# First MLP weights walked forwards and backwards, a planner that counts changes of matmul kind, and six pairs' sums on TensorE

## The chip, the cores and the metric

One core of one Trainium2 chip runs the whole program. The metric is the device time of one execution in microseconds (us), and the median over the runs is what is compared.

## The reference

Three stages follow each other. First comes soft-capped attention over 4 batches, 12 heads, 448 positions and head size 64:

```python
scores = scale * np.matmul(q, k.transpose(0, 1, 3, 2))
scores = cap * np.tanh(scores / cap)
attn = np.exp(scores - scores.max(-1, keepdims=True))
attn = attn / (attn.sum(-1, keepdims=True) + 1e-09)
attn_out = np.matmul(attn, v)
```

Then the 1792 tokens of width 768 go through a first MLP, `h = x @ w_in` (768 to 2048), `g = h * clip(h + 3, 0, 6) / 6`, `x2 = g @ w_out`. Last, each token is given to one of eight experts, greedily by its logits `x2 @ w_gate` with 224 tokens for each expert, and goes through that expert's two matrices with a relu between them.

## The kernel before, in words

The work is done in a first, planned part (attention, `x @ w_in`, the activation, the logits) and two later parts (`g @ w_out` with the routing beside it, and the experts). The change touches the planned part alone.

**Slots.** A pair is two heads of one batch; there are 24 pairs `g`, six for each batch. A slot is half a pair: two of the four chunks of 112 keys. `slot(h)` issues, for slot h: the scores (`score`, 12 matmuls of 64 rows each into the PSUM tile `sc`), the tanh and the exp on ScalarE into `P`; and for slot h-1: `av` (8 matmul instructions of 64 columns each into `po`) and `uadd`, the VectorE addition of the two chunks of `P`, which makes `u0` in the first half of a pair and `sb` in the second. For pairs from `G3 = 12` on, the second half adds `u0` as well (two additions, "whole").

**Sums and division.** Once for every two pairs, `fin_sum` multiplies `u0` and `sb` with a column block of ones (`ones`, four groups of 32 columns side by side) into the PSUM tile `ms`: 16 matmul instructions where both halves are summed on TensorE, 8 where VectorE has added them already. VectorE transposes the sums, inverts and transposes back; the result goes to DRAM (`RD`) and returns spread over the partitions (`rb`). `fin_x` multiplies the attention output `xu` by it and splits it into a high and a low part, `XH` and `XL`, which are `X[b]` of the batch. The list `FIN` says how many slots behind the two are issued (2 and 3).

**First MLP.** `m1a_pieces(b)` works through 16 tiles `f` of `w_in` in three parts of six matmuls each into `ph` (two PSUM banks). Part p needs pairs 2p and 2p+1 of `X[b]`. In batch 0 each weight tile is decoded from 64-bit numbers on VectorE (`decode`), split into a high and a low part (`wsplit`), and twelve of the sixteen (`STR`) are written to DRAM `WD` and read back by `wload` for each later batch into a ring of three buffers `ws`. The four others (`RES`) stay in `wr`. `lg_mm` sums logits from four tiles of `g` (`ms`); `wog_pieces` makes `w_out @ w_gate` on the way.

**Order.** Every operation is given to `Plan.add` with an engine, a cost and what it reads and writes; `merge` interleaves the streams by share, which fixes each operation's position. `Plan.run` then emits the program: each engine takes, among the operations that are ready by the costs, the one of the lowest position. `LAG = 6` is the number of slots by which a batch's MLP follows its attention. The engines' queues, SyncE's DMA queue too, run in the order emitted.

Of the kernel before, what the change touches and what calls it, by code (L numbers as in the profile page):

```python
# [33 lines left out]
class Plan:  # L34
# [6 lines left out]
    HOP = 0.15  # L41
    LAND = 2.0
# [15 lines left out]
    def add(self, eng, cost, fn, r=(), w=(), kb=0, after=()):  # L58
# [7 lines left out]
        for key in w:  # L66
# [5 lines left out]
            if own not in self.first:  # L72
                self.first[own] = me
                if name in self.rings:
                    deps.update(self.users.get((name, i - self.rings[name]), ()))
                    if i > 0:
                        deps.add(self.first[name, i - 1])
# [6 lines left out]
        self.ops.append((eng, cost, fn, deps, kb))  # L84
# [5 lines left out]
    def run(self):  # L90
# [12 lines left out]
        total = wire = 0.0  # L103
        for _ in range(n):
# [8 lines left out]
            _, cost, fn, _, kb = self.ops[i]  # L113
            ready[eng].remove(i)
            free[eng] = t + cost
            end = t + cost
# [14 lines left out]
def fused_kernel(ctx: ExitStack, tc: tile.TileContext, q, k, v, cap, w_in, w_out, w_gate, w1, w2,  # L131
# [22 lines left out]
    ones = cst.tile([CP + 1, 32], F32, name="ones")  # L154
    nc.gpsimd.memset(ones, 1.0)
    SB = []
    for i in range(2):
        SB.append(cst.tile([CP + 1, 2, S], F32, name=f"sb{i}"))
    guard = cst.tile([CP + 1, 1], F32, name="guard")[96:CP + 1]
# [30 lines left out]
                 "xu": 3, "ms": 1, "R": 2, "r14": 1, "rb": 2, "X": 2, "wraw": 2, "wy": 2, "ws": 3, "wot": 1, "ph": 2, "r": 1,  # L190
# [35 lines left out]
    def score(h):  # L226
# [15 lines left out]
        add("PE", 1.5, mm, r=[("KH", g), ("KL", g), ("QH", g), ("QL", g)], w=[("sc", 4 * g + c) for c in cc])  # L242
# [9 lines left out]
    G3 = 12  # L252

    def uadd(h):
# [6 lines left out]
        def go():  # L261
            u = SB[g % 2] if s_ else put(ap_, key, [CP, 2, S])
            T[key] = u
            if s_ and g >= G3:
                nc.vector.tensor_add(u[:CP], T["u0", g], T["P", 4 * g + 2])
                nc.vector.tensor_add(u[:CP], u[:CP], T["P", 4 * g + 3])
            else:
                nc.vector.tensor_add(u[:CP], T["P", 4 * g + 2 * s_], T["P", 4 * g + 2 * s_ + 1])
# [4 lines left out]
    def av(h):  # L273
# [12 lines left out]
        add("PE", 1.8, mm, r=[("tv", g)] + [("P", 4 * g + c) for c in cc], w=[("po", g)])  # L286
# [10 lines left out]
    def fin_sum(g):  # L297

        m, i = plan.next("ms"), g // 2
        halves = (1,) if g >= G3 else (0, 1)  # L300

        def mm():
            p = bank(("ms", m))
            for s_ in halves:
                for n in range(4):
                    u = T[("u0", "sb")[s_], g - 1 + n // 2]
                    r = CP + s_
                    nc.tensor.matmul(p[32 * n:32 * n + 32, :S], ones[:r], u[:r, n % 2], start=(s_ == halves[0]), stop=(s_ == 1))
        add("PE", 0.85 * len(halves), mm, r=[(("u0", "sb")[n], x) for n in halves for x in (g - 1, g)] + [("guard", 0)], w=[("ms", m)])
# [9 lines left out]
        add("DVE", 1.35, rec, r=[t], w=[R])  # L319
# [27 lines left out]
    def slot(h):  # L347
# [3 lines left out]
        av(h - 1)  # L351
        for t, fn in FIN:
# [3 lines left out]
        uadd(h - 1)  # L356
# [6 lines left out]
    FIN = ((2, fin_sum), (3, lambda g: fin_x(g - 1)), (3, fin_x))  # L363
# [21 lines left out]
    def wog_pieces():  # L385
# [8 lines left out]
        def tr(f, part):  # L394
# [11 lines left out]
            def out_():  # L406
                if i == 0 and part == 0:
                    put(dcp, ("wot", q_), [128, KD, 512])
                nc.scalar.activation(T["wot", q_][:, d0:dn, i * 128:(i + 1) * 128],
                                     T["ms", m][:, :(dn - d0) * 128].rearrange("p (d f) -> p d f", f=128), AF.Copy)  # L410
            add("ACT", 0.5, out_, r=[("ms", m)], w=[("wot", q_, f, part)])

        def mm(q_):
            m, m2 = plan.next("ms"), plan.next("ms")

            def go():
                p = bank(("ms", m))
                for d in range(KD):
                    for i in range(4):
                        nc.tensor.matmul(p[32 * i:32 * i + 32, :128], wgt[:, d, :],  # L420
                                         T["wot", q_][:, d, i * 128:(i + 1) * 128], start=(d == 0), stop=(d == KD - 1))
            add("PE", 1.0, go, r=[("wot", q_), ("wgt", 0)], w=[("ms", m)])
            c = ("wot", q_, "c")
            add("DVE", 0.3, lambda: nc.vector.tensor_copy(T["wot", q_][:, 0, :128], T["ms", m][:, :128]), r=[("ms", m)], w=[c])
            add("PE", 0.2, lambda: nc.tensor.transpose(bank(("ms", m2))[:, :128], T["wot", q_][:, 0, :128], ident),
# [6 lines left out]
        for f in range(NF):  # L432
            for part in range(len(PARTS)):
                r.append((300, lambda f=f, part=part: tr(f, part)))
            if f % 4 == 3:
                r.append((1500, lambda q_=f // 4: mm(q_)))
        return r

    W = {}

    def wput(f, key):
        if f in WD:
            T[key] = [m1p.tile([128, KD, 128], F32R, name="ws" + n, bufs=3) for n in "hl"]
        else:
            T[key] = [m1p.tile([128, KD, 128], F32R, name=f"wr{n}{f}", bufs=1) for n in "hl"]

    def wload(b, f):
        if f in WD:
            W[f] = key = ("ws", plan.next("ws"))

            def go():
                wput(f, key)
                for i in range(2):
                    nc.sync.dma_start(T[key][i].bitcast(F32), WD[f][i])
            add("SP", 0.7, go, r=[("WD", f)], w=[key], kb=768)

    def wsplit(f):

        y = decode(w_in[f], [128, KD, 128], lambda t: t)
        W[f] = key = ("ws", plan.next("ws")) if f in WD else ("wr", f)  # L460

        def high():
            wput(f, key)
# [8 lines left out]
    def lg_mm(b, tiles, first, pool):  # L472
# [6 lines left out]
        add("PE", 0.9, mm, r=[g for _, g in tiles] + [("wog", tiles[0][0] // 4)], w=[("ms", m)])  # L479
# [49 lines left out]
    def m1a_pieces(b, logits):  # L529
        gs = {}  # L530

        def mm(f, part):
            key = ("ph", NF * b + f)
            if part == 0 and f + 2 < NF:
                wload(b, f + 2) if b else wsplit(f + 2)
# [13 lines left out]
            add("PE", 1.24, go, r=xs + [w], w=[key])  # L549
            if part < 2:  # L550
                return
            n = NF * b + f
# [670 lines left out]
```

## Time and profile before

| | us |
|---|---|
| median of three runs | 1034.09 (1032.96 to 1037.63) |
| profiled execution, its own time | 1036.34 |
| its span, first to last instruction | 1034.6 |
| planned part, to the first matmul of `g @ w_out` | 473.9 |

The profile's time axis starts with the first instruction. "Busy" is the time in which an engine has an instruction under way; a TensorE matmul stays on record for longer than it holds up the next, so starts tell more than durations. The granted clock is a share of 2.4 GHz. "PE" is TensorE's matmul, "PEld" its weight load, "DVE" VectorE, "ACT" ScalarE, "SPq" SyncE's DMA queue. A release "<-" names what ended an idle time.

### The profile page before, as it was taken

The numbers are of one execution on the slowest core, as the hardware profiler recorded it, in microseconds if no ns is written. First come the engines' busy times: TensorE is split into PE (matmuls) and PEld (weight loads), VectorE is DVE, ScalarE is ACT, GpSimd is POOL, SyncE is SP. The second block draws the span as 40 slices with busy tenths as digits, with TensorE's granted clock in tenths as the row PEclk, the third lists the DMA queues.
The fourth block names the chain that finished last, engine by engine and source line by source line (L and its number), as shares of the span: only waits on it lengthen the run. The fifth ranks groups of instructions, "written<-read, shape, count | busy, mean of one in ns | idle before, by whom it ended". The sixth has DMA issues, their size and how long they took to land.

```text
span 1034.6 us, 17381 instructions
## 1 busy us (share of the span) xinstructions
PE 996.5 (96%) x6337; PEld 819.0 (79%) x6337; DVE 740.7 (72%) x1318; ACT 510.9 (49%) x868; POOL 133.0 (13%) x146
## 2 busy tenths in 40 slices
PE   6988999999999999999999999999989999999997
PEld 3434667676756678878789989998979999999996
DVE  6999888687776545447898779877337777777673
ACT  7988877776767633432110101010136665566652
POOL 0000000000000000000000000000024555545542
PEclk9999999999999999999999999999999999999999
DMA  7577999999987679996445646547948777667760
GB/s 221 154 238 237 302 342 312 382 333 318 357 286 228 199 232 339 343 315 194 151 139 141 170 108 180 135 138 226 317 170 271 232 232 242 227 223 235 244 225 29
DMA packets 120182, 242.26 MB, mean 234 GB/s; under 512 B 23392, under 2 KB 85904, under 8 KB 120096
## 3 DMA queue, kind: packets, MB, share of 16 engines
q1 hardware_dynamic: 115504, 225.08, 65.7%
q0 software_dynamic: 3328, 11.01, 3.9%
q10 hardware_dynamic: 1264, 5.05, 1.5%
q8 instruction: 50, 0.82, 0.3%
q14 instruction: 36, 0.29, 0.1%
HBM read 181.19 MB, written 59.91 MB: 233 GB/s over the span
## 4 chain that ended last, share of the span: by engine, by line
PE 70%; DVE 17%; DMA 7%; issue 3%; ACT 1%; SPq 1%; POOLq 0%; ACTq 0%; POOL 0%; DVEq 0%
PE py L1128 13%; PE x L1011 12%; PE ph L1083 7%; PE ph L545 7%; PE ph L547 6%; PE ph L546 6%; PE po L284 4%; DVE g L832 4%; PE ph L1085 4%; PE sc L241 3%; DVE g L830 3%; DMA wraw<-in_moe_w_in 1%; PE ro L840 1%; DMA gh<-gh 1%; PE ms L478 1%
## 5 line engine op out<-in xcount | busy, mean ns | idle before, releaser
L1011 PE MATMUL x<-woh,gh 128*128 128x384 f32 x448 | 125.4, 342 | 2.0 <-DMA gh<-gh 2.0
L1011 PE MATMUL x<-wol,gh 128*128 128x384 f32 x448 | 123.2, 336 | 0.0
L1011 PE MATMUL x<-woh,gl 128*128 128x384 f32 x448 | 122.2, 336 | 0.0
L545 PE MATMUL ph<-XH,wsh 128*128 128x448 f32 x288 | 110.6, 384 | 1.5 <-DMA wsh<-wd 1.2
L547 PE MATMUL ph<-XH,wsl 128*128 128x448 f32 x288 | 105.6, 367 | 0.5 <-DMA wsl<-wd 0.5
L546 PE MATMUL ph<-XL,wsh 128*128 128x448 f32 x288 | 105.3, 366 | 0.0
L245 ACT ACTIVATE P<-sc,rcap 112x896 f32<-112x896 f32 x96 | 92.2, 1005 | 12.4 <-PE sc L241 9.3
L249 ACT ACTIVATE P<-P,capt 112x896 f32<-112x896 f32 x96 | 95.6, 1045 | 0.0
L284 PE MATMUL po<-P,tv 112*64 112x448 f32 x384 | 84.3, 559 | 5.6 <-ACT P L245 3.2
L1011 PEld LDWEIGHTS x<-woh,gh 128*128 128x128 f32 x448 | 80.2, 188 | 5.8 <-DMA gh<-gh 2.9
L1011 PEld LDWEIGHTS x<-woh,gl 128*128 128x128 f32 x448 | 81.5, 188 | 1.0 <-issue 0.6
L1011 PEld LDWEIGHTS x<-wol,gh 128*128 128x128 f32 x448 | 81.5, 188 | 0.6 <-issue 0.6
L554 ACT ACTIVATE r<-ph,three 128x448 f32<-128x448 f32 x64 | 40.6, 634 | 73.2 <-PE ph L547 73.2
L545 PEld LDWEIGHTS ph<-XH,wsh 128*128 128x128 f32 x288 | 54.1, 188 | 27.3 <-issue 18.4
L556 DVE SCALAR_TENSOR_TENSOR g<-r,ph 128x448 f32<-128x448 f32 x64 | 39.5, 618 | 41.3 <-ACT r L554 41.2
L832 DVE TENSOR_SCALAR g<-mrb,m 112x1344 bf16<-112x1344 f32 (+11 forms) x105 | 68.5, 664 | 0.0
L1083 PE MATMUL ph<-xe,woh 128*128 128x448 f32 x186 | 60.8, 383 | 1.4 <-DVE xe L1069 1.0
L1105 DVE SCALAR_TENSOR_TENSOR hl<-ht,hh 128x224 fp32r<-128x224 f32 x64 | 39.9, 624 | 29.3 <-ACT hh L1104 27.9
L284 PEld LDWEIGHTS po<-P,tv 112*64 112x64 f32 x384 | 23.5, 137 | 46.1 <-issue 27.5
L748 POOL IOTA icol<- 112x112 f32 x1 | 0.2, 230 | 461.3 <-PE ph L546 461.3
L547 PEld LDWEIGHTS ph<-XH,wsl 128*128 128x128 f32 x288 | 54.1, 188 | 5.9 <-DMA wsl<-wd 1.2
L546 PEld LDWEIGHTS ph<-XL,wsh 128*128 128x128 f32 x288 | 54.2, 188 | 3.7
(211 smaller groups left out, 2243.9 us busy)
## 6 DMA issues: line engine op xcount, KB each, us to landing
wol<-in_moe_w SPq DMA_DIRECT2D x32, 768.0 KB
woh<-in_moe_w SPq DMA_DIRECT2D x31, 768.0 KB
gh<-gh SPq DMA_DIRECT2D x64, 224.0 KB
gl<-gl SPq DMA_DIRECT2D x64, 224.0 KB
wsh<-wd SPq DMA_DIRECT2D x36, 384.0 KB
wsl<-wd SPq DMA_DIRECT2D x36, 384.0 KB
wraw<-in_moe_w_in SPq DMA_DIRECT2D x16, 768.0 KB
wraw<-in_moe_w_out SPq DMA_DIRECT2D x16, 768.0 KB
```

Of the source, the lines that this page charges most:

```text
L245: add("ACT", 0.96, lambda i=i: nc.scalar.activation(put(ap_, ("P", i), [CP, 2, S]), T["sc", i][:CP, :, :S], AF.Tanh, scale=rcap[:CP]), r=[ ...
L249: add("ACT", 0.99, lambda i=i: nc.scalar.activation(T["P", i], T["P", i], AF.Exp, scale=capt[:CP]), r=[("P", i), ("capt", 0)], w=[("P", i)])
L284: nc.tensor.matmul(T["po", g][64 * j:64 * j + 64, :S], T["tv", g][:, j, c, :], T["P", 4 * g + c][:, j], start=(c == 0), stop=(c == NC - 1))
L545: nc.tensor.matmul(p, wh[:, d], XH[:, d], start=(d == 0), stop=False)
L546: nc.tensor.matmul(p, wh[:, d], XL[:, d], start=False, stop=False)
L547: nc.tensor.matmul(p, wl[:, d], XH[:, d], start=False, stop=(d == KD - 1))
L554: add("ACT", 0.64, lambda: nc.scalar.activation(put(m1p, r_, [128, S]), T[key][:, :S], AF.Relu, bias=three), r=[key], w=[r_])
L832: nc.vector.tensor_scalar(g[:, s_:], mr[:, s_:], mj, None, op0=OP.is_le)
L1011: nc.tensor.matmul(X2[g, i, hf][:, :HW], a, w[:, hf * HW:(hf + 1) * HW], start=bool(f == 0 and first), stop=bool(f == NF - 1 and last))
L1083: nc.tensor.matmul(p[:, :2 * TE], wh[:, d, fs], X2[:, d].rearrange("p a t -> p (a t)"), start=(d == 0), stop=False)
L1085: nc.tensor.matmul(p[:, :TE], wl[:, d, fs], X2[:, d, 0], start=False, stop=(d == KD - 1))
L1128: nc.tensor.matmul(PY[e][2 * t + hf][:CP, :384], a[:, f, tsl], w[:, f % 2, hf * 384:(hf + 1) * 384], start=bool(f == 0 and first), stop=bo ...
```

## The change

1. **Weights by turns.** `order(b)` walks the tiles forwards in even batches and backwards in odd ones. The last three streamed tiles of a batch stay in their buffers, which are now three named ones (`ws0` to `ws2`) handed out from a list `FREE`; a load is issued when a buffer's tile was used for the last time (`wused`). Each later batch loads 9 streamed tiles and not 12. `wog_pieces` goes backwards too, and the logits of batch 1 follow their tiles by two matmul parts fewer.
2. **Planner.** Operations on TensorE carry a kind: 0 for the MLP and the transposes, 1 for scores, 2 for `av`, 3 for sums and logits. A change of kind costs `TURN`; an operation of the kind now running (or any of kinds 1 to 3 while one of these runs) goes first if its position is less than `KEEP` behind the lowest one ready. The costs of TensorE's operations are lowered to leave the change out.
3. **Sums of six pairs on TensorE.** For pairs 0 to 5 (`G0 = 6`) `uadd` adds nothing on VectorE: for each slot four matmuls (eight instructions) of `ones` with the two chunks of `P` go straight into two of the four column groups of `ms`, which gathers two pairs over four slots. `G3` goes from 12 to 6, so pairs 6 to 11 have their third addition on VectorE and half the sum matmuls.
4. **Guard.** The small addend of the denominator is no longer an extra row of `sb`, but is added to the transposed sums.
5. **Positions.** `FIN` is 1 slot for all three steps, `LAG` is 3, and `uadd` is issued before them. The pool `late` is closed at `turn_att`.

```diff
+    TURN = 0.19
+    KEEP = 40
...
-                    i = min(i for i in c if at[i] <= t)
+                    now = [i for i in c if at[i] <= t]
+                    i = min(now)
+                    if eng == "PE" and self.ops[i][5] != was:
+                        same = [x for x in now if self.ops[x][5] == was or (was and self.ops[x][5])]
+                        if same and min(same) < i + self.KEEP:
+                            i = min(same)
...
+            if eng == "PE":
+                cost += self.TURN * (kind != was)
+                was = kind
...
-        add("PE", 1.5, mm, r=[("KH", g), ("KL", g), ("QH", g), ("QL", g)], w=[("sc", 4 * g + c) for c in cc])
+        add("PE", 1.2, mm, kind=1, r=[("KH", g), ("KL", g), ("QH", g), ("QL", g)], w=[("sc", 4 * g + c) for c in cc])
...
-    G3 = 12
+    G3 = 6
+    G0 = 6
+    MS = {}
...
+        if g < G0:
+            n0 = 2 * (g % 2)
+            if h % 4 == 0:
+                MS[g // 2] = ("ms", plan.next("ms"))
+            m = MS[g // 2]
+
+            def mm():
+                p = bank(m) if h % 4 == 0 else T[m]
+                for c in (2 * s_, 2 * s_ + 1):
+                    for j in range(2):
+                        nc.tensor.matmul(p[32 * (n0 + j):32 * (n0 + j) + 32, :S], ones, T["P", 4 * g + c][:, j],
+                                         start=(c == 0), stop=(c == NC - 1))
+            add("PE", 1.5, mm, kind=3, r=[("P", 4 * g + 2 * s_), ("P", 4 * g + 2 * s_ + 1)], w=[m])
+            return
...
-            nc.vector.reciprocal(r, y[:, :, 0])
+            nc.vector.tensor_scalar(r, y[:, :, 0], guard, None, op0=OP.add)
+            nc.vector.reciprocal(r, r)
...
-    FIN = ((2, fin_sum), (3, lambda g: fin_x(g - 1)), (3, fin_x))
+    FIN = ((1, fin_sum), (1, lambda g: fin_x(g - 1)), (1, fin_x))
...
+    def wused(b, f):
+
+        if f not in WD:
+            return
+        o = [x for x in order(b) if x in WD]
+        n = o.index(f)
+        if b < B - 1 and n >= len(o) - 3:
+            return
+        FREE.append(int(W[f][0][2:]))
+        if b and n + 3 < len(o):
+            wload(o[n + 3])
...
-    add("DVE", 1.6, guards, r=[("gexp", 0)], w=[("guard", 0)])
...
-    LAG = 6
+    LAG = 3
```

## Rows read from the trace of the kernel before

**Rows 1.** The page's first part: busy time, share of span, instructions of each engine.
```profile
PE 996.5 (96%) x6337; PEld 819.0 (79%) x6337; DVE 740.7 (72%) x1318; ACT 510.9 (49%) x868; POOL 133.0 (13%) x146
```

**Rows 2.** Windows by stretch: length, each engine's busy us (instructions), granted clock, DMA share.
```profile
4.50:23.50 19.00, 14.80 (x72) 6.74 (x72) 14.83 (x26) 15.16 (x18) 0.00 (x0) 0.94 0.82 257
23.50:59.00 35.50, 33.57 (x214) 15.74 (x212) 32.87 (x52) 33.07 (x39) 0.00 (x0) 0.98 0.55 169
59.00:104.00 45.00, 38.91 (x235) 20.43 (x234) 42.50 (x63) 39.41 (x52) 0.00 (x0) 1.00 0.76 235
104.00:364.00 260.00, 256.32 (x1631) 177.42 (x1630) 192.92 (x287) 191.45 (x281) 0.00 (x0) 1.00 0.89 307
364.00:474.00 110.00, 106.90 (x549) 86.08 (x547) 50.58 (x81) 40.49 (x66) 1.63 (x12) 1.00 0.86 299
```

**Rows 3.** Timeline of TensorE, 305 to 310 us: start, us, line, tiles, count.
```profile
305.69 0.36 PE L546 MATMUL ph<-XL,wsh 128*128 128x448 f32 x1
305.89 0.37 PE L547 MATMUL ph<-XH,wsl 128*128 128x448 f32 x1
306.19 0.46 PE L241 MATMUL sc<-QH,KH 64*112 64x448 f32 x2
306.48 0.37 PE L241 MATMUL sc<-QH,KL 64*112 64x448 f32 x2
...
307.59 1.72 PE L284 MATMUL po<-P,tv 112*64 112x448 f32 x8
309.24 0.96 PE L308 MATMUL ms<-sb,ones 113*32 113x448 f32 x8
```

**Rows 4.** Timeline, 27 to 29 us: one `fin_sum` of two halves and the next score.
```profile
27.11 0.96 PE L308 MATMUL ms<-u,ones 112*32 112x448 f32 x8
...
27.89 0.94 PE L308 MATMUL ms<-sb,ones 113*32 113x448 f32 x8
...
28.76 0.46 PE L241 MATMUL sc<-QH,KH 64*112 64x448 f32 x2
```

**Rows 5.** Timeline of TensorE, 9 to 12 us: the first change of kind.
```profile
10.88 1.41 PE L284 MATMUL po<-P,tv 112*64 112x448 f32 x6
```

**Rows 6.** Timeline of TensorE, 470 to 475 us: the last change of kind.
```profile
473.52 0.65 PE L497 MATMUL ms<-ident,lacc 128*112 128x128 f32 x4 [0.86 <-DVE lacc L487]
```

**Rows 7.** Timeline of all engines and SyncE's queue, 56 to 88 us.
```profile
56.19 1.98 ACT L249 ACTIVATE P<-P,capt 112x896 f32<-112x896 f32 x2
...
63.30 1.08 DVE L268 TENSOR_TENSOR sb<-P 112x896 f32<-112x896 f32 x1
...
66.32 0.96 PE L308 MATMUL ms<-u,ones 112*32 112x448 f32 x8
...
69.06 0.67 DVE L311 STREAM_TRANSPOSE R<-ms 128x448 f32<-128x448 f32 x1
...
77.91 1.11 SPq L329 DMA_DIRECT2D rb<-rd  x2
```

**Rows 8.** Timeline of VectorE: the last piece of `X[0]`.
```profile
86.82 0.62 DVE L345 TENSOR_TENSOR XL<-xu,XH 128x448 fp32r<-128x448 f32 x1
```

**Rows 9.** Groups by line on VectorE, 5 to 104 us: busy, mean ns, idle before.
```profile
L268 DVE TENSOR_TENSOR u<-P 112x896 f32<-112x896 f32 x10 | 10.7, 1070 | 0.0
...
L378 DVE SCALAR_TENSOR_TENSOR wy<-wraw,wy 128x768 int32<-128x768 int32 x10 | 9.6, 964 | 0.3
```

**Rows 10.** Groups by line on TensorE, 59 to 104 us: the largest idle time.
```profile
L241 PE MATMUL sc<-QL,KH 64*112 64x448 f32 x32 | 6.3, 386 | 3.7 <-DVE QL L223 3.7
```

**Rows 11.** TensorE's waits from 104 to 480 us: us, times, longest.
```profile
PE ms L403 <- DVE wy L378: 2.6, 2, 1.8
PE ph L545 <- DMA wsh<-wd: 1.2, 1, 1.2
...
PE ph L547 <- DMA wsl<-wd: 0.5, 2, 0.3
```

**Rows 12.** DMA issues by line: count, KB each.
```profile
wsh<-wd SPq DMA_DIRECT2D x36, 384.0 KB
```

More of the change, by code (lines that the diff above doesn't have):

```diff
@@ L56, in next, with add @@
         return n
-    def add(self, eng, cost, fn, r=(), w=(), kb=0, after=()):
+    def add(self, eng, cost, fn, r=(), w=(), kb=0, after=(), kind=0):
         me = len(self.ops)
@@ L83, in add @@
         deps.discard(me)
-        self.ops.append((eng, cost, fn, deps, kb))
+        self.ops.append((eng, cost, fn, deps, kb, kind))
         return me
@@ L103, in run @@
         total = wire = 0.0
+        was = 0
         for _ in range(n):
@@ L112, in run @@
             t, i, eng = best
-            _, cost, fn, _, kb = self.ops[i]
+            _, cost, fn, _, kb, kind = self.ops[i]
             ready[eng].remove(i)
-            free[eng] = t + cost
-            end = t + cost
+            if eng == "PE":
+                cost += self.TURN * (kind != was)
+                was = kind
+            end = free[eng] = t + cost
             if kb:
@@ L306, in mm @@
                     u = T[("u0", "sb")[s_], g - 1 + n // 2]
-                    r = CP + s_
-                    nc.tensor.matmul(p[32 * n:32 * n + 32, :S], ones[:r], u[:r, n % 2], start=(s_ == halves[0]), stop=(s_ == 1))
-        add("PE", 0.85 * len(halves), mm, r=[(("u0", "sb")[n], x) for n in halves for x in (g - 1, g)] + [("guard", 0)], w=[("ms", m)])
+                    nc.tensor.matmul(p[32 * n:32 * n + 32, :S], ones, u[:, n % 2], start=(s_ == halves[0]), stop=(s_ == 1))
+        if g >= G0:
+            add("PE", 0.75 * len(halves), mm, kind=3, r=[(("u0", "sb")[n], x) for n in halves for x in (g - 1, g)], w=[("ms", m)])
         t, R = ("R", 2 * i), ("R", 2 * i + 1)
@@ L478, in mm @@
                 nc.tensor.matmul(p[32 * i:32 * i + 32, :S], wog[:, f, :], T[g], start=True, stop=True)
-        add("PE", 0.9, mm, r=[g for _, g in tiles] + [("wog", tiles[0][0] // 4)], w=[("ms", m)])
+        add("PE", 0.75, mm, kind=3, r=[g for _, g in tiles] + [("wog", tiles[0][0] // 4)], w=[("ms", m)])
         key = LN[b]
@@ L532, in mm @@
         def mm(f, part):
[L533 to L535 removed]
+            x = order(b).index(f)
+            key = ("ph", NF * b + x)
+            if part == 0 and b == 0 and f + 2 < NF:
+                wsplit(f + 2)
             w = W[f]
@@ L571, in lg @@
                 LN[b] = ("lacc", plan.next("lacc"))
-            lg_mm(b, [(f, gs[f]) for f in range(4 * f4, 4 * f4 + 4)], f4 == 0, lambda: m1p)
+            lg_mm(b, [(f, gs[f]) for f in sorted(order(b)[4 * f4:4 * f4 + 4])], f4 == 0, lambda: m1p)
         r = []
-        for f in range(NF):
+        for x, f in enumerate(order(b)):
             for part in range(3):
                 r.append((1240, lambda f=f, part=part: mm(f, part)))
-                if logits and part == 1 and f % 4 == logits - 1 and f > 3:
-                    r.append((810, lambda f=f: lg(f // 4 - 1)))
+                if logits and part == 1 and x % 4 == logits - 1 and x > 3:
+                    r.append((810, lambda x=x: lg(x // 4 - 1)))
         end = []
```

108 lines of the change are left out of this document (56 added, 52 removed).

## The prediction

> **What bounds the kernel now.** I read the engines' busy shares first, then the windows by stretch, then TensorE's own timeline, and last who waited for whom. TensorE is busy for 96% of the span [rows 1]; the other engines have room on the whole, so a saving on VectorE or in DMA counts only where TensorE stands still for it. The windows show where that is [rows 2]. After 474 us nothing is edited, and I take what follows as it is. From 104 to 474 us TensorE idles for 6.8 of 370 us: only less work on it shortens that. Before 104 us it idles 4.2, 1.9 and 6.1 us in three stretches, while VectorE is busy for 42.5 of 45 us in the last of them.
>
> Recorded idle is too little, since a matmul stays on record longer than it holds up the next. So I price TensorE's work by starts. MLP matmuls follow each other at 0.20 us, score pairs at the same pace; from the last MLP matmul to the first score it is 0.30, and from the first score pair to the second 0.29 [rows 3]. A change of kind thus costs about 0.09 on each side, 0.19 in all. `av` takes 1.65 us to the next start, its two changes' shares included (about 0.37 for two instructions) [rows 3]; a `fin_sum` of two halves takes 1.65, the first half of it 0.78 [rows 4].
>
> With these prices the work in the stretches is: 4.5 to 23.5 us, 24 score pairs, 12 `av` pairs, 5 changes: 10.3 us, room 8.7 (part of it a half clock: 0.94 of full on average [rows 2]); 23.5 to 59, 48 score pairs, 36 `av` pairs, eight quadruples of sums, 12 MLP matmuls, 19 changes: 32.0, room 3.5; 59 to 104, 48 score pairs, 29 `av` pairs, eight quadruples, 49 MLP matmuls, 20 changes: 37.1, room 7.9. The planned part has 181 changes of kind from the first to the last [rows 5, 6]: 24 before 59 us, 20 to 104, 115 to 364, 22 after.
>
> Why is there room after 59 us? The last exp of batch 0 ends at 58.2 us, but the addition that follows it comes at 63.3, its sums at 66.3, the transpose at 69.1, the second load of the inverse at 77.9 and the last piece of `X[0]` ends at 87.4 [rows 7, 8]. Until then the MLP has two PSUM banks and must leave both unfinished, so TensorE has only scores and `av`, and these wait for VectorE (3.7 us for QL alone [rows 10]).
>
> **The change part by part.**
>
> Sums on TensorE. Twelve new operations of eight instructions each. The trace has no such operation; the nearest row is `av`, which also fills two column groups with 112 rows: 1.65 us [rows 3]. The bound below is the four-group sum, 0.78 for eight instructions [rows 4]; above, the whole 1.72 that `av` stays on record and a change, 1.9. I take 1.65, since only two groups work at a time. Three `fin_sum` go (1.65 each) and three more are halved (0.8 each).
>
> The Trainium skill speaks against this price: "TensorE: Matmul & The Clock Gate", Measured speedup vs the span model, has three column tiles of 32 gain 2.38-fold, not three. By that share of 0.79 a sum's 1.5 us of streaming would be an estimated 1.9, twelve of them 4.7 us more, and the sum below would be -1.5 us. The trace disagrees: four groups of 32 pass eight instructions in 0.78 us [rows 4] where `av` with two groups needs about 1.5 [rows 3].
>
> By stretch: to 23.5 us three slots have been through `av`, so 3 sums, 5.0 us, fit in the room of 8.7: 0. To 59 us nine more, 14.9, less two `fin_sum`, 3.3: 11.6, of which the room takes 3.5: **+8.1**. The slot is then 1.4 + 1.65 + 1.65 = 4.7 us on TensorE against some 4 us on ScalarE (a slot's exp is on record for 1.98 [rows 7], its tanh about as long), so TensorE is the bound there. From 59 to 104 us a `fin_sum` and a half less: **-2.4**; after it two halves: **-1.6**.
>
> VectorE. 12 additions of 1.07 us go [rows 9], 12.8, and the guard's fill. Six third additions come, 6.4 us, four of them (4.3) between 59 and 104. What is free before 59 us can decode the next weight tiles (four passes of up to 0.964 [rows 9], about 3.4 us each); buffers allow tiles up to 6, two more than before, so 6.8 us leave the crowded stretch against 4.3 that come. More important: no addition stands between the last exp and the sums, and the sums follow one slot earlier. From the last exp to `X[0]` it was 29.2 us (58.2 to 87.4), 21.1 of it behind the start of the sums; with the sums after one `av` (3 us) and without the decode that stood before the transpose (2 us) and the idle turns of the loads, I put it at 19. In 19 us four slots at ScalarE's pace of 4.7 us (its splits and copies counted) need 4 x 3.5 = 14 us of TensorE, and the four MLP parts that pairs 0 to 3 allow 4 x 1.22 = 4.9: it is full, and behind them the MLP is free. So of the room of 7.9 I let 7 go: **-7.0**; bounds 2 and 7.9. The moved steps issue the same DMAs on SyncE, four stores and four loads for two pairs, a slot earlier; the loads of `rb` still wait for the buffers of the pair two before.
>
> A wait that comes: the sums hold `ms` over four slots, and the next four must wait until VectorE has transposed. Behind the waiting sum stand the next score, and ScalarE behind it. A score and an `av` lie between (3 us), so only a decode in the way (2.5 us) shows, at two such places: bounds 0 and 3, taken **+0.6**.
>
> Planner. In 104 to 364 us there are 28 slots; a slot in its own group costs three changes (in, between, out), 84, and 31 of the 115 are sums, logits and transposes that stand alone or split a group. The new rule lets them gather beside scores and `av`, one change each and not two. I take 13 fewer: 13 x 0.19 = **-2.4**; bounds 0 and 31, 0 to -5.9. Two slots in one group I don't expect: the next score needs `sc` back from a tanh of nearly 2 us, and `av` covers 1.65. The waits after 104 us sum to 6.8 us in seven lines, 2.6 the largest [rows 11]; better costs and fewer loads take **-1.5**; bounds 0 and -5.
>
> Weights by turns. 36 tiles loaded become 27; with two halves of 384 KB each [rows 12] that is 6.9 MB less. But TensorE waited only 1.7 us for these loads in all [rows 11], which the -1.5 already holds. DMA is at 0.89 there [rows 2], so the relief itself is hidden behind TensorE's work; were it not, 1.7 us would be the whole of it. The guard, the pool and the direction cost nothing: small VectorE work after 104 us, where that engine idles for 67 of 260 us [rows 2].
>
> Sum: 0 + 8.1 - 2.4 - 7.0 - 1.6 + 0.6 - 2.4 - 1.5 = **-6.2 us**. Against the profiled execution, 1036.3 (span 1034.6 and 1.7 around it), that is 1030.1; that execution lies 2.2 above the median, so the forecast is **1028 us**.
>
> **The rivals.**
>
> *VectorE stays the bound from 59 to 104 us.* If its freed time is not used for decodes ahead (the loads of raw weights or the two buffers hold them), the four third additions stand in a stretch that has 2.5 us free, and `X[0]` is not earlier. The 7.0 of room stay and up to 4.3 come: +5.1, 1039. It decides from the point where VectorE's work between `X[0]`'s last exp and its last piece is not shorter than 29 us. For it: 42.5 of 45 busy. Against: 12.8 us leave just ahead.
>
> *The planner gathers more.* Changes from 104 us on near three a slot (-5.9) and waits mostly gone (-5): 7 better, 1021. For it: lone sums and logits are many; against: ready times limit it.
>
> *The new rule changes nothing* because score and `av` are adjacent in most slots already: changes stay, waits stay, 3.9 worse: 1032.
>
> *The column groups overlap poorly:* sums at 1.9 us, the bound above, give 12 x 0.25 = 3.0 more: 1031. Against it stands that the four-group sum already runs at twice the rate of `av` [rows 3, 4].
>
> **How the numbers follow.** About 0.5%, 5.2 us, can be told from no change. Forecast's case 0.42 (0.25 beyond that bound, 0.17 within it); VectorE stays the bound 0.20 (slower 0.14, same 0.06); planner gathers more 0.25, faster; the rule changes nothing 0.10 and poor overlap 0.03, the same. Faster 0.50, same 0.36, slower 0.14. The range takes in VectorE's rival and the planner's with the early room fully used: 1017 to 1040. The likeliest case alone has 1024 to 1032.
>
> **What would show it.** The window from 23.5 to 59 us, and TensorE's slots there 4.7 us apart with `ms` after each `po`; the last `XL` of batch 0 within 21 us of the last exp of slot 11 (29 before); TensorE with hardly any idle time behind that exp; some 177 changes of kind (181, 13 fewer late, nine more early), about 100 of them between `X[0]` and the last slot; 27 loads of `wsh`; 1034 - 474 = 560 us unchanged behind the planned part. Wrong it would be if `XL` still comes 29 us after that exp, if sums take more than 1.7, if attention falls so far behind the MLP that batch 3's `X` is late, or if the later part moves.

## The result and the profile after

The changed kernel takes 1028.83 us (median of 12 runs, 1025.62 to 1032.16). The kernel before, timed beside it each time, takes 1036.69 us (12 runs, 1032.96 to 1040.22). The ratio is 0.9917 (the median of the ratios run by run; the two medians alone give 0.9924), with a 95% interval of 0.9901 to 0.9932: faster by 0.8%, beyond the 0.5% that can be told. The profiled execution of the changed kernel took 1030.02 us with a span of 1028.2, against 1036.34 and 1034.6 before: -6.3 us.

The page's first part, after:

```profile
PE 1002.8 (98%) x6361; PEld 822.8 (80%) x6361; DVE 736.3 (72%) x1321; ACT 511.3 (50%) x868; POOL 133.2 (13%) x146
```

TensorE has 6 us more work on record and a span that is 6 us shorter, so the gain is idle time that was filled. The windows show where. Their cuts are shifted to the same points of the program as in [rows 2]: three slots through `av`, the end of the last exp of batch 0, the end of `X[0]`'s stretch, the end of the planned part. A line has the stretch, its length, the busy us and instructions of TensorE, its weight load, VectorE, ScalarE and GpSimd, then the granted clock, the DMA share and GB/s.

```profile
4.50:24.40 19.90, 19.09 (x96) 7.84 (x96) 14.84 (x26) 15.52 (x19) 0.00 (x0) 1.00 0.83 264
24.40:64.70 40.30, 39.06 (x232) 15.74 (x230) 36.55 (x60) 35.63 (x42) 0.00 (x0) 1.00 0.83 277
64.70:100.00 35.30, 35.30 (x206) 21.82 (x205) 27.08 (x43) 31.04 (x42) 0.00 (x0) 1.00 0.43 133
100.00:364.00 264.00, 262.94 (x1682) 183.51 (x1680) 203.76 (x306) 198.43 (x290) 0.00 (x0) 1.00 0.85 295
364.00:464.40 100.40, 98.12 (x511) 80.56 (x507) 47.25 (x76) 39.50 (x64) 1.56 (x12) 1.00 0.78 278
```

Read the second and third: the stretch with the sums has grown, from 35.5 to 40.3 us, and from 64.7 us on TensorE has no idle time at all, where it idled for 6.1 of 45 us before [rows 2]. VectorE, busy for 42.5 of 45 us there before, is now busy for 27.1 of 35.3. The planned part ends with the first matmul of `g @ w_out`, at 464.4 us (473.9 before): **-9.5 us**. What follows, which the change doesn't edit, takes 563.9 us instead of 560.6: **+3.3**.

A slot in the second stretch, on TensorE's timeline:

```profile
21.14 1.76 PE L310 MATMUL po<-P,tv 112*64 112x448 f32 x8
22.83 1.70 PE L291 MATMUL ms<-P,ones 112*32 112x448 f32 x8
24.46 0.46 PE L251 MATMUL sc<-QH,KH 64*112 64x448 f32 x2
...
27.52 1.70 PE L291 MATMUL ms<-P,ones 112*32 112x448 f32 x8
29.14 0.46 PE L251 MATMUL sc<-QH,KH 64*112 64x448 f32 x2
```

From a new sum to the next start it is 24.46 - 22.83 = 1.63 us, and from score to score 29.14 - 24.46 = 4.68.

The way from the last exp of slot 11 to `X[0]`, the steps of [rows 7, 8], in the timeline of all engines:

```profile
62.74 1.97 ACT L259 ACTIVATE P<-P,capt 112x896 f32<-112x896 f32 x2
...
67.79 1.70 PE L291 MATMUL ms<-P,ones 112*32 112x448 f32 x8
...
70.19 0.64 DVE L338 STREAM_TRANSPOSE R<-ms 128x448 f32<-128x448 f32 x1
...
72.51 1.12 SPq L351 DMA_DIRECT2D rd<-R  x4
...
73.73 1.09 SPq L357 DMA_DIRECT2D rb<-rd  x2
...
83.98 0.63 DVE L373 TENSOR_TENSOR XL<-xu,XH 128x448 fp32r<-128x448 f32 x1
```

No addition stands between the exp and the sums. The exp ends at 64.7 and the last piece of `X[0]` at 84.6: 19.9 us, not 29.2.

TensorE's waits from 100 to 480 us (us in total, times, the longest):

```profile
PE ms L528 <- DVE g L608: 1.5, 1, 1.5
PE ms L547 <- DVE lacc L537: 0.8, 1, 0.8
PE ms L431 <- DVE wog L455: 0.5, 1, 0.5
PE ms L431 <- ACT wot L437: 0.3, 1, 0.3
PE ph L596 <- DVE g L608: 0.3, 1, 0.3
```

Together 3.4 us; the wait for `wy` of 2.6 [rows 11], a decoded tile of `w_out` that came late, is gone, and so are those for split weights. The DMA issues have nine of each half, 27 tiles, where it was 36 [rows 12]:

```profile
ws2h<-wd SPq DMA_DIRECT2D x9, 384.0 KB
```

The later part shows its 3.3 us in the granted clock. For 6.8 us it is 0.50, the lower of TensorE's two levels (1.2 of 2.4 GHz):

```profile
487.00:493.80 6.80, 6.80 (x24) 5.04 (x23) 6.80 (x15) 0.00 (x0) 0.00 (x0) 0.50 0.20 60
```

The stretch that lies as far behind the end of the planned part, before:

```profile
496.60:503.40 6.80, 6.80 (x39) 6.35 (x39) 6.80 (x16) 0.00 (x0) 0.00 (x0) 1.00 0.38 98
```

24 matmuls passed where 39 had, and TensorE doesn't make that up. The windows at the same distance behind the end of the planned part, two of the kernel before and then two after:

```profile
493.90:593.90 100.00, 98.60 (x713) 87.48 (x713) 83.81 (x202) 11.66 (x23) 0.00 (x0) 1.00 0.54 152
860.00:1034.60 174.60, 166.94 (x1029) 162.17 (x1027) 117.12 (x182) 98.80 (x220) 79.73 (x79) 0.99 0.61 202
484.40:584.40 100.00, 98.00 (x693) 86.17 (x693) 82.04 (x197) 11.56 (x23) 0.00 (x0) 0.97 0.50 146
850.50:1028.20 177.70, 170.16 (x1047) 165.33 (x1045) 118.89 (x185) 100.66 (x224) 81.00 (x79) 0.99 0.61 203
```

In the first 100 us 20 matmuls fewer are done, and 18 of them are left for the last stretch, which is 3.1 us longer. The kernel before has one such stretch of 3.4 us elsewhere in its later part (768.8 us); in the 110 us around it (750 to 860 us) 636 matmuls passed, as many as after. In both kernels VectorE is busy all through the 6.8 us shown above with the compares of the routing. In front of the slow stretch TensorE had waited for them three times, 1.5 us in all (twice, 1.1 us, at that place before):

```profile
484.01 0.37 PE L885 MATMUL ro<-g,Ob 112*32 112x448 bf16 x4 [0.32 <-DVE g L877]
484.97 0.37 PE L885 MATMUL ro<-g,Ob 112*32 112x448 bf16 x4 [0.58 <-DVE g L877]
485.93 0.37 PE L885 MATMUL ro<-g,Ob 112*32 112x448 bf16 x4 [0.58 <-DVE g L877]
```

### The profile page after: what moved, and what is told of

It is laid out like the page before. It is cut to its first block, busy times and chain, and to the rows that moved or that the text cites. A ratio compares the mean times of both kernels' runs of the same rounds, so it can differ in the third digit from the quotient of the medians.

```text
span 1028.2 us, 17382 instructions
## 1 busy us (share of the span) xinstructions
PE 1002.8 (98%) x6361; PEld 822.8 (80%) x6361; DVE 736.3 (72%) x1321; ACT 511.3 (50%) x868; POOL 133.2 (13%) x146
## 2 busy tenths in 40 slices
DMA packets 117589, 235.18 MB, mean 229 GB/s; under 512 B 23104, under 2 KB 85616, under 8 KB 117504
## 4 chain that ended last, share of the span: by engine, by line
PE 79%; DVE 9%; DMA 7%; issue 2%; ACT 1%; SPq 1%; POOLq 0%; POOL 0%; ACTq 0%; DVEq 0%
PE x L1056 16%; PE py L1173 13%; PE ph L596 7%; PE ph L1128 7%; PE ph L598 7%; PE ph L597 7%; PE po L310 6%; PE sc L251 5%; PE ph L1130 3%; DVE g L877 2%; DMA gh<-gh 2%; PE ro L885 2%; PE ms L528 1%; PE ms L291 1%; DVE g L875 1%
## 5 line engine op out<-in xcount | busy, mean ns | idle before, releaser
L1128 PE MATMUL ph<-xe,woh 128*128 128x448 f32 x186 | 59.2, 376 | 1.4 <-DVE xe L1114 1.0
L899 ACT ACTIVATE cs<-ro 128x448 f32<-128x448 f32 x7 | 3.8, 547 | 108.1 <-PE ro L892 108.1
L1128 PE MATMUL ph<-xe,we 128*128 128x448 f32 x180 | 56.9, 374 | 0.0
L1173 PE MATMUL py<-we,hh 128*112 128x384 f32 x256 | 56.1, 341 | 0.0
L310 PEld LDWEIGHTS po<-P,tv 112*64 112x64 f32 x384 | 23.5, 137 | 40.3 <-issue 33.2
L1025 ACT ACTIVATE row<-x 128x384 f32<-128x384 f32 x26 | 11.7, 490 | 85.7 <-PE x L1056 72.7
L875 DVE TENSOR_SCALAR g<-mrb,m 112x112 bf16<-112x112 f32 (+5 forms) x84 | 49.7, 591 | 0.0
L1149 ACT ACTIVATE hh<-ht 128x224 fp32r<-128x224 f32 x64 | 25.1, 392 | 49.1 <-DVE ht L1148 46.2
```

Of the source, the lines that this page charges most:

```text
L310: nc.tensor.matmul(T["po", g][64 * j:64 * j + 64, :S], T["tv", g][:, j, c, :], T["P", 4 * g + c][:, j], start=(c == 0), stop=(c == NC - 1))
L875: nc.vector.tensor_scalar(g[:, :s_], mr[:, :s_], mj, None, op0=OP.is_lt)
L1128: nc.tensor.matmul(p[:, :2 * TE], wh[:, d, fs], X2[:, d].rearrange("p a t -> p (a t)"), start=(d == 0), stop=False)
L1173: nc.tensor.matmul(PY[e][2 * t + hf][:CP, :384], a[:, f, tsl], w[:, f % 2, hf * 384:(hf + 1) * 384], start=bool(f == 0 and first), stop=bo ...
```

## An account of the planned part

To compare kernels I price each trace's planned part as the prediction did: an MLP matmul or score pair 0.20 us, an `av` or new-sum pair 0.37, a pair of four-group sums 0.19, a change of kind 0.185. "Room" is the end of the planned part, less 4.5 us and less that sum; it holds idle time, slow clock and the small errors of the prices, which is why it can be just below zero. "Exp to X[0]" runs from the last exp of batch 0 to its last `XL`. Ends are those of one profiled execution each. The last column has that execution's time less the median of its kernel's runs; the runs of one kernel lie 3 to 11 us apart. So a difference of a few us between two ends is clear of chance only where the ratios of the experiments, which go by all runs, part as well.

| kernel | planned end | work with changes | changes | room before 100 / to 364 / after | exp to X[0] | later part | profiled less median |
|---|---|---|---|---|---|---|---|
| before | 473.9 | 442.8 | 181 | 20.4 / 1.4 / 4.9 | 29.2 | 560.6 | -0.4 |
| after | 464.4 | 453.6 | 179 | 5.1 / -1.2 / 2.4 | 19.9 | 563.9 | +1.2 |
| sums on VectorE | 468.2 | 439.7 | 165 | 19.8 / 1.8 / 2.3 | 25.9 | 564.1 | +0.4 |
| rule off | 470.5 | 456.8 | 197 | 4.5 / 0.7 / 3.9 | 19.8 | 562.3 | +1.7 |
| always forward | 470.3 | 453.5 | 179 | 4.4 / 4.9 / 2.8 | 19.9 | 561.5 | -2.3 |
| planner alone | 467.0 | 440.0 | 167 | 18.8 / -1.0 / 4.5 | 31.1 | 559.6 | -2.2 |
| traffic put back | 470.4 | 453.6 | 179 | 3.6 / 5.5 / 3.1 | 19.9 | 563.1 | +0.7 |
| late steps | 465.2 | 453.6 | 179 | 5.7 / -1.3 / 2.7 | 19.8 | 562.8 | +0.2 |
| four pairs | 467.0 | 447.3 | 173 | 11.5 / 1.1 / 2.7 | 22.2 | 563.8 | +2.0 |
| planner and weights | 467.1 | 440.3 | 168 | 19.9 / -0.1 / 2.4 | 25.9 | 561.1 | -5.5 |
| weights alone | 474.1 | 443.5 | 185 | 19.2 / 3.2 / 3.7 | 25.8 | 563.4 | +2.4 |
| window of 20 | 468.7 | 454.7 | 185 | 4.0 / 2.3 / 3.2 | 20.1 | 565.2 | +2.9 |
| window of 60 | 472.3 | 452.3 | 172 | 6.1 / 4.8 / 4.5 | 19.0 | 562.0 | +2.7 |
| window of 120 | 485.0 | 451.0 | 165 | 5.0 / 9.6 / 14.8 | 19.7 | 561.1 | -0.1 |

From before to after: work +10.8, room -15.3 before 100 us, -2.6 to 364 us, -2.5 behind: -9.6, the 9.5 but for rounding.

Part of the room is slow clock. Between 4.5 us and the planned end TensorE stood at 0.50 for 3.4 us once before (21.3 us), with the traffic put back (186.5, and again in its last 0.5 us), with four pairs (177.4) and with the window of 60 (184.6, and again in its last 0.9 us); twice with the sums on VectorE (21.2 and 178.2), with the planner alone (21.6 and 76.2) and with planner and weights (21.7 and 59.2); for 0.8 us with the weights alone and for 3.4 and 13.7 us with the window of 120; and not at all in the others. A stretch of 3.4 us in which TensorE is busy throughout is worth 1.7 us.

## The experiments

Each ratio is against the kernel before, with its 95% interval.

**1. Sums back on VectorE** (all else as after).

```
-    G3 = 6
-    G0 = 6
+    G3 = 12
+    G0 = 0
```

> The changed kernel with the sums of pairs 0 to 5 back on VectorE (G0 = 0, G3 = 12), all else as changed. Theory A (the prediction's: the additions on VectorE are what keeps the first X late and TensorE waiting): TensorE's matmul work falls by 11 us but its room before 104 us grows back to 15 us or more, X[0] comes more than 25 us behind the last exp of slot 11 (20 in the changed kernel, 29 before), and the planned part ends at 466 to 472 us (464.4 changed, 473.9 before). Rival B (the earlier positions of the division and the MLP give X[0] early by themselves, and the sums on TensorE only add work): X[0] within 21 us, planned part ends at 455 to 461 us, and the kernel is faster than the changed one by 4 us or more.

Measured: 1033.65 us, 0.9962 [0.9938, 0.9985]; planned end 468.2, +3.8. The windows:

```profile
24.40:60.00 35.60, 32.35 (x206) 14.37 (x204) 33.56 (x54) 32.43 (x37) 0.00 (x0) 1.00 0.53 162
60.00:100.00 40.00, 36.12 (x208) 21.94 (x206) 38.32 (x60) 31.67 (x43) 0.00 (x0) 1.00 0.77 246
```

The kernel after has 40.0 of 40 us in the second of them (its row stands in experiment 5). VectorE is back at 38.3 of 40, TensorE's idle time is back, and the room before 100 us is 19.8 as it was before: 17.7 us of room in all against 13.9 of work. So the sums pay by what they fill, 3.8 us net here, up to 3.4 of it slow clock; the ratio lies clear of the whole change's 0.9901 to 0.9932.

**2. Rule off** (the planner still knows the kinds and the price of a change, but never prefers the kind it has).

```
-    KEEP = 40
+    KEEP = 0
```

> The changed kernel with the planner's preference for the running kind taken away (KEEP = 0); the price of a change of kind stays in the costs. Theory A: some 9 to 20 changes of kind more than 179, and a few waits back: the planned part ends 2 to 5 us later than 464.4. Rival (the rule moves little, the waits after 104 us went through the costs): the number of changes within 5 of 179 and the end within 1 us of 464.4.

Measured: 1032.95 us, 0.9930 [0.9903, 0.9957]; planned end 470.5, +6.1. 18 more changes are 18 x 0.185 = 3.3 us; the other 2.8 are room, which the counting of changes alone doesn't give, and the end lies beyond the 2 to 5 us expected. The whole time doesn't show it: the ratio is 1.3 us from that of the whole change, and the intervals overlap.

**3. Weights always forward** (36 tiles loaded, each batch's first three during the batch before; `wog_pieces` goes forwards again too).

```
     def order(b):
-        return list(range(NF))[::-1 if b % 2 else 1]
+        return list(range(NF))
...
         if b and n + 3 < len(o):
             wload(o[n + 3])
+        elif b < B - 1 and n + 3 >= len(o):
+            wload(o[n + 3 - len(o)])
```

> The changed kernel with the weights walked forwards in every batch: 36 tiles loaded instead of 27, the logits' weights made in forward order; loads still by free buffer. Theory A (loads lie beside matmuls): TensorE waits for streamed weights 1 to 2 us in all, the planned part ends at 464.5 to 467 us. Rival (the DMA relief is what took the waits after 104 us away and made X earlier): the end at 469 us or later, TensorE's waits after 104 us back at 6 us or more.

Measured: 1035.92 us, 0.9975 [0.9956, 0.9994]; planned end 470.3, +5.9, with the same 179 changes. The prediction had put nothing beyond 1.7 us on this. The waits from 100 to 480 us, the largest:

```profile
PE ms L431 <- DVE wy L406: 2.9, 3, 2.3
PE ms L431 <- DVE lacc L535: 1.3, 1, 1.3
PE ms L431 <- ACT wot L437: 1.2, 2, 0.7
```

None of these is a wait for a split weight (`ws`): they stand at `L431`, the transposes of `w_out`.

**4. Planner alone** (the planner's part of the diff on the kernel before: kinds, costs, `TURN`, `KEEP`).

> The kernel before with the planner's part alone (kinds, price of a change, preference, lowered costs). Theory A: changes of kind from 181 to some 165, room before 104 us unchanged at about 20, planned part ends at 469 to 472 us (473.9 before). Rival (the planner is most of the gain): the end at 467 us or earlier. Third way (late attention): the end after 475 us, batch 3's X late.

Measured: 1030.60 us (6 runs), 0.9917 [0.9892, 0.9941]; planned end 467.0, -6.9 from before. Its 167 changes and few shifts make 2.8 us less work, and the room is 4.1 us less. The rival in the expectation, 467 or earlier, is what came: by itself the planner's part is worth more than the 3.9 us that the prediction gave it and the waits together. It is the rule and the new costs together; no run has the costs alone on the kernel before.

**5. The saved traffic put back** (after, and where each of the nine kept tiles was last used its two halves are copied from DRAM to DRAM; nothing waits for the copies, and the planner isn't told their size).

```
+            def again():
+                for i in range(2):
+                    nc.sync.dma_start(JUNK[b][f][i], WD[f][i])
+            add("SP", 0.7, again, r=[("WD", f)], w=[("junk", 16 * b + f)], after=[last])
```

> The changed kernel with the nine tile loads that were saved put back as traffic alone: where a kept tile was last used, its two halves are copied from DRAM to DRAM on the same queue, and nothing waits for the copies. The planner is told nothing of their size. Theory after the forward run (the saved loads make way for the raw w_out tiles, whose late decodes hold up transposes in TensorE's queue): the planned part ends 2 to 6 us later than 464.4, TensorE's waits on wy and wot between 100 and 300 us rise from 1 to 3 us or more. Prediction's theory (loads hidden; the forward run's 5.9 us came through the order of weights and logits): ends within 1 us of 464.4.

Measured: 1034.53 us, 0.9967 [0.9952, 0.9983]; planned end 470.4, +6.0, with the same 179 changes and the forward kernel's room within 0.8 us in each part. The page counts 242.26 MB for it, as for before, and 235.18 for after. It writes 7.07 MB more to DRAM than before, which a load to SBUF doesn't. Windows of it:

```profile
150.00:200.00 50.00, 45.14 (x295) 30.16 (x294) 38.54 (x56) 36.94 (x54) 0.00 (x0) 0.97 0.97 359
```

The same and its neighbours, after:

```profile
60.00:100.00 40.00, 40.00 (x234) 23.64 (x233) 29.73 (x48) 34.80 (x45) 0.00 (x0) 1.00 0.47 149
150.00:200.00 50.00, 48.94 (x329) 32.68 (x329) 43.55 (x63) 42.10 (x62) 0.00 (x0) 1.00 0.96 344
200.00:250.00 50.00, 50.00 (x329) 38.11 (x328) 37.55 (x58) 35.99 (x58) 0.00 (x0) 1.00 0.99 371
```

And the decode's first pass in the groups by line on VectorE, 100 to 364 us, with the traffic:

```profile
L405 DVE TENSOR_SCALAR wy<-wraw 128x768 int32<-128x768 int32 x23 | 12.8, 556 | 19.0 <-DMA wraw<-in_moe_w_out 17.6 <-DMA wraw<-in_moe_w_in 1.3 <-issue 0.2
```

after, without it:

```profile
L404 DVE TENSOR_SCALAR wy<-wraw 128x768 int32<-128x768 int32 x23 | 12.8, 558 | 9.3 <-DMA wraw<-in_moe_w_out 8.2 <-DMA wraw<-in_moe_w_in 1.1
```

DMA is at 0.96 to 0.99 from 100 to 250 us in both. With the traffic the raw `w_out` comes later: VectorE waits 17.6 us for it instead of 8.2, and TensorE is busy for 45.1 of 50 us instead of 48.9. Once the whole way is on record, from late data over a late decode to a transpose that TensorE waits for, on VectorE's and TensorE's timelines:

```profile
182.23 0.56 DVE L405 TENSOR_SCALAR wy<-wraw 128x768 int32<-128x768 int32 x1 [2.42 <-DMA wraw<-in_moe_w_out]
...
184.93 0.52 PE L432 MATMUL ms<-ident,wy 128*128 128x128 f32 x3 [1.96 <-DVE wy L407]
```

VectorE's wait for raw `w_out` doesn't tell the end by itself: it is 4.2 us before, 9.8 always forward (470.3) and 1.9 with late steps (465.2). So within the whole change the weights' gain is the traffic, not the direction of the walk, and the ratio is clear of the whole change's; which waits it goes through is shown in part only.

**6. Late steps** (after, with the closing steps of a pair and the MLP's lag where they were).

```
-    FIN = ((1, fin_sum), (1, lambda g: fin_x(g - 1)), (1, fin_x))
+    FIN = ((1, fin_sum), (3, lambda g: fin_x(g - 1)), (3, fin_x))
...
-    LAG = 3
+    LAG = 6
```

> The changed kernel with the division's last step three slots behind again and the MLP six (FIN 1, 3, 3 and LAG 6); the sums stay on TensorE one slot behind. Theory A (the additions gone make X[0] early, positions count little): X[0] 20 to 23 us behind the last exp, planned part ends at 464 to 466.5 us. Rival B (positions make X[0] early): X[0] 25 us or more behind the exp, room before 100 us from 5 to 9 us or more, end at 468 us or later.

Measured: 1029.58 us, 0.9928 [0.9905, 0.9950]; planned end 465.2, `X[0]` 19.8 us behind the exp. The earlier positions are worth 0.8 us by this, and the ratios can't tell the two kernels apart; `X[0]` isn't early because of them.

**7. Four pairs instead of six.**

```
-    G3 = 6
-    G0 = 6
+    G3 = 4
+    G0 = 4
```

> The changed kernel with the sums of pairs 0 to 3 on TensorE instead of 0 to 5 (G0 = G3 = 4). TensorE has four sums of 1.65 us less and a half-sum of 0.8 more, -5.8 us; VectorE has six additions of 1.07 more before 70 us, 6.4 us. If TensorE is the bound from slot 2 on: planned part ends at 459 to 462 us. If VectorE comes back as the bound behind the last exp: X[0] later than 23 us behind it, end at 464 to 468 us.

Measured: 1030.53 us, 0.9918 [0.9902, 0.9934]; planned end 467.0, +2.6. 6.3 us less work, but the room before 100 us is 11.5: 6.4 of the 15.3 us are back, with `X[0]` 22.2 us behind the exp, short of the 23 expected for that case. Two pairs on VectorE are enough for it to be waited for again. The whole time isn't to be told from that of six pairs.

**8 to 10. A wider and a narrower window** (how far behind the next in order an operation of the same kind may be and still be taken).

```
-    KEEP = 40
+    KEEP = 120      # 8; 20 in 9, 60 in 10
```

> The changed kernel with KEEP = 120: matmuls of the running kind may go ahead of operations up to 120 positions older. If changes are what counts: below 165 changes (179), planned part ends at 460 to 463 us. If attention falls behind: batch 3's X lands more than 8 us later than 396.9 us, TensorE waits behind 364 us, end at 466 us or later.

> The changed kernel with KEEP = 20. Between KEEP 0 (197 changes, planned part ends at 470.5) and 40 (179, 464.4): if the number of changes carries it, 183 to 190 changes and an end of 466 to 468 us. If chance positions carry it, the end is outside of 464 to 470.5.

> The changed kernel with KEEP = 60, half way to 120, where batch 3's X came 26 us later and the planned part ended at 485.0. If the loss sets in when that X is later than the MLP of batch 3 can wait: X below 410 us, 168 to 178 changes, end at 462 to 465 us. If it grows with the distance: end at 467 to 472 us.

Measured, 120: 1048.00 us, 1.0106 [1.0087, 1.0125], slower; 20: 1032.78 us, 0.9949 [0.9926, 0.9972]; 60: 1033.46 us, 0.9963 [0.9940, 0.9985]. The changes fall with the window, 197, 185, 179, 172, 165 for 0, 20, 40, 60, 120, and the planned end is 470.5, 468.7, 464.4, 472.3, 485.0. From 40 on the waits rise faster than the changes fall. The expectations for 20 and 60 hold in their changes, 185 and 172, but the ends lie above what they gave with them. By the ratios 60 and 120 are slower than 40; 0 and 20 can't be told from it. With 60, the largest from 100 to 490 us:

```profile
PE ms L431 <- DVE wy L406: 3.1, 2, 2.0
PE ph L598 <- DVE ws2l L516: 2.0, 1, 2.0
```

With 120 the MLP goes ahead of attention and runs out of work: the last `X` ends at 422.8 us (396.9 after). TensorE's timeline ahead of it:

```profile
409.25 0.96 PE L528 MATMUL ms<-g,wog 128*32 128x448 f32 x8 [0.77 <-DVE R L338]
411.40 1.62 PE L528 MATMUL ms<-gl,wog 128*32 128x448 f32 x8 [1.20 <-DVE lacc L537]
413.77 1.10 PE L547 MATMUL ms<-ident,lacc 128*112 128x128 f32 x4 [0.75 <-DVE lacc L537]
...
420.34 0.74 PE L596 MATMUL ph<-XH,ws2h 128*128 128x448 f32 x1 [1.52 <-ACT XH L371]
```

From 405.9 to 420.3 us there is no MLP matmul; the logits wait on each other's transposes, and from 411.6 us the granted clock is 0.50 for 13.7 us (an MLP matmul stands at 0.74 us on record, not 0.37).

**11. Planner and weights, without the sums** (sums on VectorE, steps late, `uadd` behind them as before).

```
-    G3 = 6
-    G0 = 6
+    G3 = 12
+    G0 = 0
...
+    FIN = ((2, fin_sum), (3, lambda g: fin_x(g - 1)), (3, fin_x))
...
+    LAG = 6
```

> The changed kernel's planner and weights by turns alone: sums of all pairs on VectorE as before (G0 = 0, G3 = 12), FIN 2, 3, 3 and LAG 6 with the additions behind them as before. If the gains of the parts add up (planner alone -6.9, weights -6 by the runs that took them away): planned part ends at 460 to 462 us, earlier than the full change's 464.4, and the sums on TensorE are no gain of their own. If each part works through the same room (a DMA-bound stretch from 100 to 250 us and a VectorE-bound one before 100): 464 to 468 us, room before 100 us near 19 us.

Measured: 1035.41 us, 0.9976 [0.9956, 0.9996]; planned end 467.1, that of the planner alone (467.0). But this profiled execution is the fastest of the twelve, 5.5 us below their median, and the ratio lies apart from the planner alone's 0.9892 to 0.9941: over all runs, the planner with the weights by turns and without the sums is some 6 us slower than the planner alone. Why isn't shown.

**12. Weights alone** (as 11, with `KEEP = 0`).

> As planner_weights, with the preference for the running kind off too (KEEP = 0; the costs stay the new ones): the weights by turns nearly alone. If the saved traffic is a gain of its own: planned part ends at 467 to 470 us (473.9 before), TensorE's waits on wy after 104 us below 1 us (2.6 before). If it counts only beside the new rule: 472 to 475 us.

Measured: 1036.85 us, 0.9986 [0.9967, 1.0004]; planned end 474.1, that of before (473.9): by themselves the weights by turns are worth nothing that can be told. TensorE waited 1.5 us for `wy`, not below 1. Experiments 11 and 12 differ in the rule alone, as do the whole change and experiment 2: 17 changes and 7.0 us of planned end here, 18 and 6.1 there, but only 1.0 and 1.3 us by the ratios, within the intervals.

## Why the prediction was right, and where it was not

The forecast was 1028 us, and 1030.1 for the profiled execution, which took 1030.02. The sum's -6.2 us is -6.3 there and -7.9 by the medians. The planned part and the later part are off by 3.3 us each, in opposite directions, so the closeness of the total is partly luck.

**Price of a sum: right.** 1.65 taken, 1.63 measured, with the change of kind in it. The rival of poor overlap, at 1.9, falls. By the Trainium skill's 2.38-fold gain for three column tiles ("TensorE: Matmul & The Clock Gate", Measured speedup vs the span model) the prediction had also estimated 1.9 us for the streaming alone; the trace doesn't bear that out. It doesn't test the 2.38 itself: the estimate started from an `av` that already uses two groups, and no run passes such data through one group alone.

**The stretch to 104 us: right, by its mechanism and its size.** The prediction let the sums fill 5.0 + 3.5 us of room and gave 7.0 more to the earlier `X[0]`: 15.5 of 20.1. Measured: 15.3 of 20.4. The slot is 4.68 us (4.7), `X[0]` comes 19.9 us behind the exp (19), and TensorE has no idle time behind that exp. Experiments 1 and 7 show that VectorE's additions made the room: it is back with all of them and 6.4 us of it with two pairs. So VectorE's rival falls. Not all of `X[0]`'s 9.3 us are the sums': with the additions on VectorE it comes 25.8 to 25.9 us behind the exp (experiments 1, 11, 12), 3.3 us nearer than before, and which other part gives that isn't shown. The new wait for `ms`, 0.6 taken, shows as one of 1.2 us in TensorE's waits from 4 to 104 us:

```profile
PE ms L291 <- DVE R L338: 1.2, 1, 1.2
```

**Changes of kind: right in number.** 13 fewer were expected behind that stretch; from 100 us on there are 128, not 139: 11 fewer, 2.1 us. In all it is 179 (177 expected). Between `X[0]` and the last slot it is 117, 125 before, not the about 100 named: the late changes fell partly behind the last slot and less in the middle than I had them. That the rule changes nothing falls by the count: without it there are 197 (experiment 2). What these changes are worth in time stands on single executions (experiments 2, 11, 12).

**Waits behind 104 us: too small, and the reason was wrong.** -1.5 was taken, with -5 as its bound; the room there fell by 5.1, and TensorE's waits on record from 6.8 to 3.4 us. The step that failed is that the relief of the DMA "is hidden behind TensorE's work", with 1.7 us as "the whole of it". Experiments 3 and 5 both take away 6 us of the gain (6.0 and 5.2 by the ratios), one by loading the tiles again and one by moving the same bytes to nowhere. I had looked for the loads' cost in the waits for the loads themselves [rows 11], and there it isn't. Where it is, is open in part. Experiment 5 has a stall of 2.0 us behind late raw `w_out`. But of the 2.6 us for `wy` before [rows 11], which are gone after, the longer wait, 1.8 us to 254.2 us, has no late data in front of it: its decode stood in VectorE's queue right behind two additions (VectorE's timeline before, the second of them and the first pass of the decode):

```profile
250.47 1.09 DVE L266 TENSOR_TENSOR sb<-sb,P 112x896 f32<-112x896 f32 x1
251.48 0.55 DVE L376 TENSOR_SCALAR wy<-wraw 128x768 int32<-128x768 int32 x1
```

The longest wait of experiment 3, 2.3 us to 196.6 us, has no wait for raw data just in front of its decode either. The first stretches had also been taken as if they left the later ones alone. But that transfers were put off from there doesn't come out of the windows: the DMA share from 60 to 100 us is 0.47 (0.73 before), up to 60 us it is 0.81 (0.63 before), and from 150 to 200 and to 250 us 0.96 and 0.99 (0.96 and 0.94 before). Why less traffic helps in the whole change (experiment 5) and not without the sums (11, 12) is open. The planner's rival had both its terms part of the way: -2.1 of -5.9, and all of the -5.

**The later part: wrong as "unchanged".** It took 563.9 us, not 560.6, and the prediction had named that as a way to be wrong. The 6.8 us at half clock cost half their length, 3.4 us, and that is the 3.3: counted from the end of the planned part, TensorE's 100th matmul starts at the same time in both kernels, the 200th 3.6 us later after, and the last 3.3 us later. The stretch of 3.4 us before cost next to nothing. In the fourteen kernels' profiles this part, the same program in all, takes 559.6 to 565.2 us, with slow stretches at other places; the four that have none up to TensorE's last matmul take 559.6 to 562.3. The profiled execution has the lowest mean granted clock of the changed kernel's twelve (0.994; 0.995 to 0.998 in the others). What brings such a stretch on is left open.

**The parts don't add.** By the ratios the whole is worth 8.6 us. Taken away alone, the sums cost 4.7 us and the traffic 5.2, both clear of the whole's interval; the rule costs 1.3 and the positions 1.1, which can't be told from nothing (3.8, 6.0, 6.1 and 0.8 by the planned ends). Put in alone, the planner's part gives 8.6, as much as the whole, and the weights nothing that can be told; planner and weights together give 2.5, less than the planner alone. That they draw on the same waits, so that what one part fills another can't fill again, would fit; it doesn't explain the loss by the weights without the sums. By their ratios the planner alone (0.9917) can't be told from the whole change (0.9917), nor can four pairs (0.9918); the change has the earliest planned end of all that ran, by 2.6 us against each of these two, and no kernel here beat it. Whether its planned part would show fully with a later part as short as the planner's (559.6) isn't shown.

One choice was poor: I took 2.2 us off the forecast because the profiled execution lay above the median of three runs. With twelve runs the median before is 1036.69, and the profiled execution lies on it. These 2.2 us and the 1.7 us by which the gain was forecast too small (6.2, and 7.9 by the medians) nearly cancel, so 1028 against 1028.83 is luck too.

## What to carry to other kernels

When the busiest engine idles for a few per cent, moving work onto it can shorten the span, if that work is what another engine is late with just there: price the added work and the room it fills in the same stretch. A DMA saving isn't judged by the waits for the saved transfers: here they were 1.7 us, and putting the same bytes back as traffic alone cost 5 to 6, so that is the run to make. A planner's rule that groups like work needs its window tried: 60 and 120 were slower than 40 here. And an end read from one profiled execution is to be held against all runs: by the ends the weights added nothing to the planner, by the runs they cost some 6 us.

## What the runs showed of the hardware

Eight instructions of 112 rows in two column groups take the same time for a 32-wide sum as for the 64-wide `av`: 1.63 us to the next start (after, 22.83 us) and 1.65 (before [rows 3]), with the change of kind in it.

A half-clock stretch of TensorE stood behind short stalls in a part where it was otherwise busy: 6.8 us from 487.0 us, behind three waits of 1.5 us in all (after), 3.4 us at 186.5 us in the kernel with the traffic put back, just behind waits of 2.0 and 1.0 us, and 13.7 us at 411.6 us behind waits of about 2 us with no MLP work (window of 120). A stall doesn't always bring one: with the rule off, TensorE waited at the same place of the later part three times, 1.6 us in all, and the granted clock stayed at 1.00. The 6.8 us, in which TensorE was busy throughout, cost the later part half their length, which it didn't make up; the 3.4 us at 768.8 us before cost it next to nothing.
